# A scan and a mixture of adapters on one core: stores of two chunks in 4 KB rows, x stepped over the pair, fillers on TensorE, and new orders of all queues

## The chip, the cores and the metric

The kernel runs on one core of a Trainium2 chip. The metric is device time in microseconds (us) of one launch: the median of several runs. Five queues of instructions run beside each other and meet only through semaphores: PE (TensorE: matmuls, transposes), ACT (ScalarE), DVE (VectorE), POOL (GpSimd) and SP, which issues nearly all transfers. The transfers themselves run on 16 DMA engines.

## The reference

Two parts follow each other. The first is a linear recurrence along time, for 8 sequences of 6400 steps and 128 channels:

```python
for t in range(S):
    h = a[:, t] * h + b[:, t]
    out[:, t] = h
```

Its result, seen as 51200 tokens x of 128 numbers, goes through a mixture of 8 adapters of rank 16. A gate picks the two best adapters of each token, weighs them by a softmax over the two logits, and adds what they give:

```python
logits = x @ w_gate                          # 51200 x 8
topk = the two largest of each row; w = softmax of those two
delta[token] = sum over the two of w * ((x @ A[e]) @ B[e])
return x + delta
```

All inputs and the output are float32. a, b and the output have 26.2 MB each, so 78.6 MB have to pass between HBM and SBUF.

## The kernel before, in words

**Tiles.** The 51200 tokens are cut into 100 chunks of 512 tokens; a chunk has 4 blocks of 128 tokens. Loads fetch two chunks at a time (512 KB each for a and for b; the first four chunks come alone). A paired load gives each of the 128 partitions 8 tokens that follow each other in HBM, a row of 4 KB; a store of two chunks gives each partition 4 tokens of one chunk and 4 of the other, so it writes rows of 2 KB.

**One chunk's way.** Its steps carry short names in the planner, which also stand in this text:
- `la`, `lb`: loads of a and b (line 707), into rings of 6 pairs.
- `A`, `B`, `P` (line 728): PE transposes tokens into channels x time, in PSUM. `P` does b of one chunk and a of the next at once, with half of the rows of the array each.
- `ae` (line 746): ACT copies the transposed a to SBUF. `sc` (line 784): DVE runs the recurrence along the free axis and writes x, in half precision, to a ring of 24 chunks. These four are the front.
- `Z` (line 804): PE multiplies x with A and w_gate, in units of mostly 6 blocks. x is the weight operand: column 4p+j of a chunk belongs to partition p and block j, so the 128 weights of a block stand four halves apart. `ze` (line 810): ACT copies that to SBUF.
- Gating, in groups of mostly 4 units, on DVE, POOL and ACT (lines 841 to 880): the two largest logits, a sigmoid, the weights `g`.
- `mu` (line 913 on POOL, `md`, line 917, on DVE): z times the gate weights. `T` (line 926): PE transposes that. `te` (line 935 on DVE, 932 on ACT): a copy to SBUF. `D` (lines 940 and 941): PE adds x, again as weights with a step of four, and z B in PSUM. `oe` (line 955 on ACT, `od`, line 952, on DVE): a copy to the output ring of 18 chunks. `st` (line 986): SP stores a pair. These are the back.

**What sets the order.** Each engine works its own list from front to end and waits at an instruction until what that needs is done. The lists come from a planner in the kernel's file: each operation has an estimated duration and a wished-for time (the table `NUDGE`, one number for each operation), and the planner orders each engine's operations by that. Lists like `TE_ACT`, `MU_DVE` and `OE_DVE` say which of two engines does a step:

```python
rank[op.i] = op.base + TEMPLATE... + NUDGE.get(op.name, 0.0)
queue = {e: sorted((o for o in self.ops if o.eng == e), key=lambda o: (rank[o.i], o.i)) for e in self.ENGINES}
```

Fronts run ahead of backs, by some 16 to 20 chunks in the middle of the run. Loads stand ahead of stores on SP: the last load, `lb98`, is issued when stores up to `st62` have been issued, and the rest of the stores follow it. At the start PE transposes the identity 16 times (`wu`, line 611); the table `FILL`, for more such work before some fronts, is empty.

Of the kernel before, what the change touches and what calls it, by code (L numbers as in the profile page):

```python
# [10 lines left out]
PERIOD = 6  # L11
FREE = {"pe": 0.0, "act": 0.105, "dve": 0.082, "pool": 0.044, "sp": 0.0}
SEEN = {"pe": 0.06, "act": 0.04, "dve": 0.055, "pool": 0.08, "sp": 0.0}
SELF = {"pe": 0.0, "act": 0.035, "dve": 0.035, "pool": 0.078, "sp": 0.0}
PE_WAIT = 0.08
PE_FREE = 0.1
SP_MARGIN = 2.0
LAND_MARGIN = 1.0
Q_RATE = {3: 4.2e-3, 5: 2.1e-3, 7: 2.1e-3}
SCAN_SELF = 0.13  # L20
ISSUE = {"sp": 0.52, "act": 0.45}
LOAD_RATE = 387e3
STORE_RATE = 413e3
DMA_START = 0.3
DMA_SEEN = 1.15
DMA_DEPTH = 9
FIRST_ISSUE = 0.7
FIRST_WORK = 0.73
TABLES = 1.32
NUDGE = {  # L30
# [182 lines left out]
}  # L213
WINDOW = {'pe': 0.0, 'act': 0.0, 'dve': 0.0, 'pool': 0.0, 'sp': 0.0}
START = (-999, "", 0)
FIRST = -9999
EARLY = -400
LEAD = [1, 2]
# [4 lines left out]
FLAT = []  # L223
FILL = {}
# [70 lines left out]
class Program:  # L295
# [5 lines left out]
    def __init__(self):  # L301
        self.ops = []
# [802 lines left out]
```

## Time and profile before

| what | number |
|---|---|
| median of 3 runs | 202.84 us (202.61 to 203.44) |
| span of the profiled execution, first to last instruction | 200.9 us; the page gives no other time of that execution |
| busy: PE, DVE, ACT, POOL | 177.7, 176.2, 175.8, 136.9 us |
| moved between HBM and SBUF | 52.56 MB read, 26.21 MB written |
| packets on the main queue | 28456 |

The span lies 1.9 us under the median of the runs: it leaves out what is done around the program. Busy times of PE are modelled, and a busy PE is not PE at its peak. The DMA share can be over 1, as packets of one engine overlap.

### The profile page before, as it was taken

What the parts mean: (1) busy time and instruction counts of PE and PEld (TensorE: products, weight loads), DVE (VectorE), ACT (ScalarE), POOL (GpSimd) and SP (SyncE); (2) the same over time, 40 slices, a digit from 0 to 9 for tenths busy, and PEclk for the clock granted to TensorE, in tenths of its full rate; (3) what the DMA queues carried; (4) which work ended last, traced back from release to release, by engine and by line L of the source; (5) the groups of instructions that cost most, each with busy time, mean ns of one, the idle gap of its engine ahead of it and who ended that gap; (6) DMA issues with size and microseconds to landing.
All of it is one profiled execution on the core that took longest, in us unless ns stands there. A gap on an engine that the chain in (4) does not pass through costs nothing.

```text
span 200.9 us, 7611 instructions
## 1 busy us (share of the span) xinstructions
PE 177.7 (88%) x3192; PEld 155.9 (78%) x3192; DVE 176.2 (88%) x283; ACT 175.8 (88%) x327; POOL 136.9 (68%) x176
## 2 busy tenths in 40 slices
PE   6888978999899969999988999899999997898970
PEld 6766867888688858888878888787888886787860
DVE  1699999999999968999897999798899998999971
ACT  2589998999779969999997999899999998899970
POOL 1331559498989887797987797868876466767420
PEclk9999999999999999999999999999999999999998
DMA  6999999999999999999999999999999999999985
GB/s 216 378 412 408 411 405 401 411 406 404 414 409 400 412 416 409 401 417 407 409 413 409 410 409 412 413 410 411 417 408 410 414 410 409 406 381 387 357 338 215
DMA packets 29065, 79.26 MB, mean 395 GB/s; under 512 B 2664, under 2 KB 2920, under 8 KB 29032
## 3 DMA queue, kind: packets, MB, share of 16 engines
q1 hardware_dynamic: 28456, 78.39, 99.0%
q8 instruction: 25, 0.41, 0.8%
q10 hardware_dynamic: 576, 0.40, 0.7%
q14 instruction: 8, 0.07, 0.1%
HBM read 52.56 MB, written 26.21 MB: 392 GB/s over the span
## 4 chain that ended last, share of the span: by engine, by line
DMA 33%; PE 27%; DVE 16%; ACT 15%; SPq 5%; issue 2%; DVEq 0%; ACTq 0%
DMA a_tm<-in_a_dram 26%; DVE xT L784 9%; DMA out_dram<-outt 7%; ACT zl L810 5%; PE pZ L804 5%; SPq L707 5%; PE pB L728 5%; PE pA L728 5%; ACT outt L955 4%; PE pO L940 4%; PE pO L926 4%; ACT a_st L746 4%; PE pO L941 3%; DVE zwT L935 2%; ACT zwT L932 2%
## 5 line engine op out<-in xcount | busy, mean ns | idle before, releaser
L784 DVE TENSOR_TENSOR_SCAN xT<-a_st,xT,pB 128x512 f16<-128x512 f32 x96 | 120.4, 1254 | 7.1 <-PE pA L728 4.3
L913 POOL TENSOR_TENSOR zw<-zl,g 128x512 f16<-128x512 f32 x88 | 92.7, 1067 | 27.9 <-DVE g L880 19.6
L728 PE MATMUL pB<-ident_f,b_tm 64*128 64x64 f32 (+1 forms) x784 | 69.3, 229 | 6.8 <-DMA a_tm<-in_a_dram 6.7
L728 PE MATMUL pA<-ident_f,a_tm 64*128 64x64 f32 (+1 forms) x784 | 69.8, 230 | 0.5 <-DMA b_tm<-in_b_dram 0.3
L746 ACT COPY a_st<-pA 128x512 f32<-128x512 f32 x100 | 63.3, 638 | 4.1 <-PE pA L728 3.3
L728 PEld LDWEIGHTS pB<-ident_f,b_tm 64*128 64x128 f32 (+1 forms) x784 | 56.4, 139 | 11.8 <-DMA a_tm<-in_a_dram 8.3
L810 ACT COPY zl<-pZ 128x816 f32<-128x816 f32 (+1 forms) x69 | 59.7, 865 | 2.0 <-PE pZ L804 1.7
L728 PEld LDWEIGHTS pA<-ident_f,a_tm 64*128 64x128 f32 (+1 forms) x784 | 56.8, 139 | 5.6 <-issue 0.4
L955 ACT COPY outt<-pO 128x512 f32<-128x512 f32 x88 | 55.9, 640 | 3.9 <-PE pO L941 3.0
L940 PE MATMUL pO<-ident_h,xT 128*128 128x128 f16 x368 | 51.6, 222 | 1.3 <-ACT zwT L932 1.0
L941 PE MATMUL pO<-cst_h,zwT 128*128 128x128 f16 x368 | 50.5, 219 | 0.0
L940 PEld LDWEIGHTS pO<-ident_h,xT 128*128 128x128 f16 x368 | 40.2, 113 | 4.3 <-ACT zwT L932 1.4
L804 PE MATMUL pZ<-cst_h,xT 128*128 128x136 f16 x400 | 35.9, 225 | 4.9 <-DVE xT L784 2.0
L941 PEld LDWEIGHTS pO<-cst_h,zwT 128*128 128x128 f16 x368 | 36.8, 100 | 0.0
L926 PE MATMUL pO<-ident_h,zw 128*128 128x128 f16 x368 | 35.2, 220 | 1.4 <-ACT outt L955 1.1
L804 PEld LDWEIGHTS pZ<-cst_h,xT 128*128 128x128 f16 x400 | 26.3, 114 | 9.1 <-DVE xT L784 4.3
L926 PEld LDWEIGHTS pO<-ident_h,zw 128*128 128x128 f16 x368 | 22.9, 97 | 4.7 <-ACT outt L955 1.3
L935 DVE COPY zwT<-pO 128x512 f16<-128x512 f16 x57 | 22.9, 407 | 4.0 <-PE pO L926 3.7
L932 ACT COPY zwT<-pO 128x512 f16<-128x512 f16 x35 | 21.9, 630 | 4.7 <-PE pO L926 4.3
L850 POOL TENSOR_TENSOR L<-k,m 128x192 f32<-128x192 f32 (+2 forms) x16 | 8.4, 524 | 6.2 <-DVE m L848 6.1
L872 POOL TENSOR_TENSOR k<-k,L 128x192 f32<-128x192 f32 (+1 forms) x17 | 9.4, 556 | 4.3 <-DVE L L868 3.0
L846 POOL TENSOR_TENSOR L<-L,k 128x192 f32<-128x192 f32 (+1 forms) x15 | 8.6, 576 | 5.4 <-DVE L L843 4.7
(58 smaller groups left out, 112.2 us busy)
## 6 DMA issues: line engine op xcount, KB each, us to landing
a_tm<-in_a_dram SPq DMA_DIRECT2D x48, 512.0 KB, 13.3
b_tm<-in_b_dram SPq DMA_DIRECT2D x48, 512.0 KB, 13.5
out_dram<-outt SPq DMA_DIRECT2D x47, 512.0 KB, 13.4
a_tm<-in_a_dram SPq DMA_DIRECT2D x4, 256.0 KB, 4.3
out_dram<-outt SPq DMA_DIRECT2D x4, 256.0 KB, 3.6
b_tm<-in_b_dram SPq DMA_DIRECT2D x3, 256.0 KB, 5.1
out_dram<-outt SPq DMA_DIRECT2D x1, 496.0 KB
b_tm<-in_b_dram ACTq DMA_DIRECT2D x1, 256.0 KB, 3.4
```

Source lines behind the costliest of these rows:

```text
L728: last = eng["pe"].transpose(*args)
L746: lambda: eng["act"].copy(a_st[c % NA][:, :], pA[:, c % 2, :]), fr(c, "ae"))
L784: last = eng["dve"].tensor_tensor_scan(out=x[:, s0:s1], data0=a_st[c % NA][:, s0:s1], data1=pB[:, c % 2, s0:s1], initial=init, op0=ALU.mul ...
L804: last = eng["pe"].matmul(pZ[:, k // (n // 2), o : o + W], xblock(b0 + k), Awg_h)
L810: return eng["act"].copy(zl[:, zb : zb + n, :].rearrange("p (h k) w -> p h (k w)", h=2), pZ[:, :, 0 : n // 2 * W])
L913: lambda: eng["pool"].tensor_tensor(out=wv, in0=zv, in1=gv, op=ALU.mult), ba(gi, c, "mu"))
L926: last = eng["pe"].transpose(ptile[:, k * 128 : k * 128 + 128], zz[:, k, :], ident_h[:, :])
L932: lambda: eng["act"].copy(zt, ptile[:, 0 : n * 128]), ba(gi, c, "ta"))
L935: lambda: eng["dve"].tensor_copy(zt, ptile[:, 0 : n * 128]), ba(gi, c, "te"))
L940: eng["pe"].matmul(dst, xblock(b0 + k), ident_h[:, :], start=True, stop=False)
L941: last = eng["pe"].matmul(dst, zt[:, k * 128 : k * 128 + 128], B_h, start=False, stop=True)
L955: lambda: eng["act"].copy(ov, bv), ba(gi, c, "oe"))
```

## The change

The planner, its estimates, `NUDGE` and its switches go away. The order of each of the five lists is written out by name in a table `ORDER`, and the engine of a step is the one in whose list its name stands. Instructions, sizes of rings and units stay but for the points below; names of gate operations are `g` on every engine, and `mu`, `te`, `oe` on every engine.

```diff
-FILL = {}
+FILL = {k: 4 for k in range(7, 15)}
 ...
-            dst = out[r0 : r0 + m * C, :].rearrange("(h p j) d -> p h j d", p=128, j=J)
-            view = outt[:, q : q + m * J, :].rearrange("p (h j) d -> p h j d", j=J)
+            dst = out[c * C : (c + m) * C, :].rearrange("(p j) d -> p j d", p=128)
+            view = outt[:, q : q + m * J, :]
 ...
         def xblock(b):
-            return xcols(b // J).rearrange("d (p j) -> d j p", j=J)[:, b % J, :]
+            s0, n = tile_of[b // J]
+            o = s0 % NX * C
+            return xT[:, o : o + n * C].rearrange("d (p j) -> d j p", p=128)[:, b - s0 * J, :]
```

- **Stores.** A store of two chunks writes, from each partition, 8 tokens that follow each other: 128 rows of 4 KB instead of 256 of 2 KB. The last four chunks are still stored alone. Stores now use 16 semaphores in turn.
- **x over the pair.** For that, block j of a pair must hold the tokens 8p+j of its 1024. So the weights of `Z` and `D` are taken with a step of eight halves over the x of both chunks. `Z` therefore waits for the scan of the pair's second chunk, and the x of a pair is free again when `D` of both chunks has run.
- **Fillers.** Before the paired transposes that make a of chunks 7 to 14, PE transposes the identity four times into the place where that a goes:

```diff
+        def filler(c):
+            def f(e):
+                for _ in range(FILL[c]):
+                    last = e.transpose(pA[:, c % 2, 0:128], ident_f[:, :], ident_f[:, :])
+                return last
+            if c in FILL:
+                o_fi[c] = P.add("pe", f"fi{c}", FILL[c], get(o_ae, c - 2) + [o_id], f)
```

- **Orders.** All five lists are new. From SP's: near the start, and around the last load:

```diff
+    "sp": (
+        "la0 lb1 la1 la3 lb2 la2 lb3 la4 lb4 la6 lb6 ... la16 lb16 la18 lb20 lb18 la20 la24 la22 st0 lb22 ... "
+        "... st58 lb96 st60 la98 st62 st72 st64 lb98 st66 st68 st78 st76 st70 st74 st82 ... st94 st96 st97 st98 st99"
```

PE's end and those of ACT and DVE, from the last paired transpose `P98`, the last copy of a (`ae99`) and the last scan (`sc99`) on:

```diff
+    "pe":  "... T82 Z65 T83 D82 D83 T84 P98 T85 D84 Z66 D85 T86 B99 T87 Z67 T90 D86 ... D97 T99 D98 D99"
+    "act": "... te83 oe82 ze65 oe83 ae99 te85 oe84 ze66 oe85 w1_17 te86 te87 ... w1_21 te97 oe96 oe97 oe98 oe99"
+    "dve": "... mu88 sc98 g6_18 g7_17 mu90 g2_18 g8_17 sc99 mu94 te91 te88 gx_19 ... mu98 g8_21 mu99 te98 te99"
```

Before, the same places were: PE `P98 D83 D82 Z65 B99 T85 T84 Z66 ...`, ACT `oe83 oe82 ze65 ae99 ze66 oe85 ...`, DVE `sc98 te85 te84 g4_17 sc99 g1_18 g7_17 ...`.

By the two tables, DVE has 62 `te` (60 before), 5 `oe` (7), 10 `mu` (12) and ten gate operations more; ACT has 38 `te` (40) and 95 `oe` (93); POOL has 90 `mu` (88) and ten gate operations fewer.

More of the change, by code (lines that the diff above doesn't have):

```diff
@@ L302, in __init__, with add @@
         self.ops = []
-    def add(self, eng, name, dur, deps, emit, at, sem=None, locks=False, parts=1):
+        self.where = {name: e for e in ORDER for name in ORDER[e].split()}
+    def add(self, may, name, n, deps, emit, sem=None, parts=1):
         op = Op()
         op.i = len(self.ops)
-        op.eng, op.name, op.dur, op.emit = eng, name, dur, emit
-        op.base, op.kind, op.k = at
-        op.deps = [d for d in deps if d is not None]
-        op.sem, op.locks = sem, locks or eng == "pool"
-        op.cnt, op.clock, op.parts = 0, None, parts
+        op.may = may.split()
+        op.eng = self.where.get(name, op.may[0])
+        assert op.eng in op.may
+        op.name, op.n, op.emit = name, n, emit
+        op.deps = deps
+        op.sem, op.cnt, op.clock, op.parts = sem, 0, None, parts
@@ L393, in schedule @@
+    def schedule(self):
+        named = {op.name: op for op in self.ops}
+        assert len(named) == len(self.ops)
+        self.order = {e: [named[name] for name in ORDER[e].split()] for e in self.ENGINES}
+        assert sum(len(o) for o in self.order.values()) == len(self.ops)
         for e in self.ENGINES:
@@ L398, in schedule, with waits @@
                     op.cnt = n
-    def waits(self, sems, dma_sems):
+    def waits(self):
         dma_cnt = {}
@@ L411, in waits @@
                     op = self.order[e][at[e]]
-                    if any(d.clock is None for d, _ in op.deps):
+                    if any(d.clock is None for d in op.deps):
                         break
@@ L475, in bass_associative_scan_2x2__then__mixture_of_adapters_kernel @@
     NU = len(units)
-    GMAX = 4
-    stores = []
-    c0 = 0
-    for n in [2] * ((NCH - sum(STORE_TAIL)) // 2) + STORE_TAIL:
+    stores, tile_of, c0 = [], {}, 0
+    for n in STORES:
         stores.append((c0, n))
+        assert c0 % NX + n <= NX and c0 * J % NO + n * J <= NO
+        for c in range(c0, c0 + n):
+            tile_of[c] = (c0, n)
         c0 += n
     assert c0 == NCH
-    groups = []
-    u0 = 0
-    for n in LEAD + [GMAX] * ((NU - sum(LEAD) - sum(TAPER)) // GMAX) + TAPER:
+    groups, u0 = [], 0
+    for n in GROUPS:
         groups.append((u0, n))
@@ L490, in bass_associative_scan_2x2__then__mixture_of_adapters_kernel @@
     assert u0 == NU
-    bbase = []
-    for u0, n in groups:
-        e = (units[u0 + n - 1][0] + units[u0 + n - 1][1]) // J - PERIOD
-        bbase.append(max(e, bbase[-1] + PERIOD * last / GMAX) if bbase else e)
-        last = n
-    gfirst = [units[u0][0] // J for u0, n in groups]
     glast = [(units[u0 + n - 1][0] + units[u0 + n - 1][1]) // J - 1 for u0, n in groups]
@@ L552, in bass_associative_scan_2x2__then__mixture_of_adapters_kernel @@
         outt = sbuf("outt", [128, NO, 128], F32)
-        GB = GMAX * U
+        GB = max(sum(m for _, m in units[u0 : u0 + n]) for u0, n in groups)
         m1 = sbuf("m1_", [128, GB], F32, 2)
@@ L600, in bass_associative_scan_2x2__then__mixture_of_adapters_kernel @@
-        o_sg = P.add(
-            "act", "sg", TABLES + 0.2, [(o_id, True)],
-            lambda: eng["act"].activation(warm[:, :], ident_f[:, 0:E], ACTF.Sigmoid), START,
-        )
-        o_ih = P.add(
-            "dve", "ih", 0.25, [(o_id, True)],
-            lambda: eng["dve"].tensor_copy(ident_h[:, :], ident_f[:, :]), START,
-        )
-        o_wu = []
-        for k in range(WARM):
-            o_wu.append(P.add("pe", f"wu{k}", 0.218 if k < WARM0 else 0.109, [(o_id, True)],
-                  lambda: eng["pe"].transpose(pO[:, 0, 0:128], ident_f[:, :], ident_f[:, :]),
-                  START if k < WARM0 else (0, "wu", 0)))
@@ new lines, in bass_associative_scan_2x2__then__mixture_of_adapters_kernel @@
+        P.add("act", "sg", 0, [o_id], lambda e: e.activation(warm[:, :], ident_f[:, 0:E], ACTF.Sigmoid))
+        o_ih = P.add("dve", "ih", 0, [o_id], lambda e: e.tensor_copy(ident_h[:, :], ident_f[:, :]))
+        o_wu = [
+            P.add("pe", f"wu{k}", 0, [o_id],
+                  lambda e: e.transpose(pO[:, 0, 0:128], ident_f[:, :], ident_f[:, :]))
+            for k in range(WARM)
+        ]
+        o_ch = P.add("dve", "ch", 0, o_c[1:], lambda e: e.tensor_copy(cst_h[:, 128:], cst_f[:, 128:]))
@@ L727, in f @@
                     for args in group:
-                        last = eng["pe"].transpose(*args)
+                        last = e.transpose(*args)
                 return last
@@ L748, in front @@
-        def front(c):
-            r0 = rows[c]
-            o_fi = []
-            for k in range(FILL.get(c, 0)):
-                o_fi.append((P.add(
-                    "pe", f"fi{c}_{k}", 0.109, [(o_id, True)] + get(o_sc, c - 2),
-                    lambda: eng["pe"].transpose(pB[:, c % 2, 0:128], ident_f[:, :], ident_f[:, :]), fr(c, "fi")), True))
+            o_ae[c] = P.add("act", f"ae{c}", J, [o_A[c]] + get(o_sc, c - NA),
+                            lambda e: e.copy(a_st[c % NA][:, :], pA[:, c % 2, :]))
@@ new lines, in load_next, with f @@
+        def load_next(c):
+            if c < NCH and c not in o_la:
+                load(c, 1 if c < HEAD else HC)
+        o_fi = {}
+        def filler(c):
+            def f(e):
+                for _ in range(FILL[c]):
[3 more added lines that the diff above has]
+                o_fi[c] = P.add("pe", f"fi{c}", FILL[c], get(o_ae, c - 2) + [o_id], f)
+        def front(c):
+            load_next(c)
@@ L853, in maxes @@
-            def maxes():
-                for k in range(nb):
-                    last = eng["dve"].max(out=t8[:, k, :], in_=Lp[:, k, :])
-                return last
-            def first():
-                return eng["dve"].tensor_reduce(out=v1, in_=Lp, axis=X, op=ALU.max)
-            d1 = P.add("dve", f"g1_{gi}", 0.09 + 0.075 * nb if top else 0.142 + nb * E * 1.04e-3,
-                       [(o_ze[u], True) for u in range(u0, u0 + n)] + old, maxes if top else first, ga(gi, "g1"))
+                return P.add("dve" if kind == 8 else "pool dve", f"g{kind}_{gi}", nb, deps, f)
@@ L863, in gating @@
+            top = nb <= TOP8
+            ready = [o_ze[u] for u in range(u0, u0 + n)] + old
             if top:
+                t8 = v8[s][:, 0:nb, :]
                 b1, b2 = (t8[:, :, k : k + 1].to_broadcast([128, nb, E]) for k in (0, 1))
-                d2 = wide(2, [(d1, True)] + old,
-                          lambda e: e.tensor_tensor(out=kk, in0=Lp, in1=b1, op=ALU.subtract))
-                d5 = wide(6, [(d1, True)] + old,
-                          lambda e: e.tensor_tensor(out=ll, in0=Lp, in1=b2, op=ALU.subtract))
-            else:
-                d2, d5 = search()
@@ L871, in gating, with maxes @@
-            d6 = wide(7, [(d2, True), (d5, True)],
-                      lambda e: e.tensor_tensor(out=kk, in0=kk, in1=ll, op=ALU.add))
-            a1 = P.add("act", f"w1_{gi}", 0.19 + nb * E * 0.86e-3, [(d6, True)] + old,
-                       lambda: eng["act"].activation(sg, kk, ACTF.Sigmoid), ga(gi, "w1"))
+                def maxes(e):
+                    for k in range(nb):
+                        last = e.max(out=t8[:, k, :], in_=Lp[:, k, :])
+                    return last
+                d1 = P.add("dve", f"gx_{gi}", nb, ready, maxes)
@@ L875, in gating @@
+            d6 = wide(7, [d2, d5], lambda e: e.tensor_tensor(out=kk, in0=kk, in1=ll, op=ALU.add))
+            a1 = P.add("act", f"w1_{gi}", nb, [d6] + old, lambda e: e.activation(sg, kk, ACTF.Sigmoid))
             for u in range(u0, u0 + n):
@@ L899, in back_part @@
-        def back_part(gi, ch, c, b0, n):
             u0 = groups[gi][0]
+            b0 = c * J
             q0 = b0 - units[u0][0]
             w = c % NW
-            us = [u for u in range(u0, u0 + groups[gi][1]) if units[u][0] < b0 + n and units[u][0] + units[u][1] > b0]
-            gv = g[gi % NG][:, q0 : q0 + n, :].unsqueeze(3).broadcast_to([128, n, E, R])
+            us = [u for u in range(u0, u0 + groups[gi][1]) if units[u][0] < b0 + J and sum(units[u]) > b0]
+            gv = g[gi % NG][:, q0 : q0 + J, :].unsqueeze(3).broadcast_to([128, J, E, R])
@@ L918, in back_part @@
-            for k in range(n):
+            zv = zl[:, zp : zp + J, 0:128].rearrange("p q (e r) -> p q e r", e=E)
+            zz, zt = zw[w], zwT[w][:, :]
+            wv = zz[:, :, :].rearrange("p q (e r) -> p q e r", e=E)
+            o_mu[c] = P.add("pool dve", f"mu{c}", J, [o_ze[u] for u in us] + [o_g[gi]] + get(o_T, c - NW),
+                            lambda e: e.tensor_tensor(out=wv, in0=zv, in1=gv, op=ALU.mult))
+            for k in range(J):
                 zlast[zp + k] = o_mu[c]
@@ L922, in back_part @@
             ptile = bank.bitcast(F16)
-            def tr():
-                for k in range(n):
-                    last = eng["pe"].transpose(ptile[:, k * 128 : k * 128 + 128], zz[:, k, :], ident_h[:, :])
-                return last
-            o_T[c] = P.add("pe", f"T{c}", 0.1 + 0.056 * n, [(o_mu[c], True), (o_ih, True)] + free + [(o, True) for o in (o_wu if c < 2 else [])], tr, ba(gi, c, "T"))
-            if te_act(c):
-                o_te[c] = P.add("act", f"te{c}", 0.165 + 0.107 * n, [(o_T[c], True)] + get(o_D, c - NW),
-                                lambda: eng["act"].copy(zt, ptile[:, 0 : n * 128]), ba(gi, c, "ta"))
-            else:
-                o_te[c] = P.add("dve", f"te{c}", 0.14 + 0.0672 * n, [(o_T[c], True)] + get(o_D, c - NW),
-                                lambda: eng["dve"].tensor_copy(zt, ptile[:, 0 : n * 128]), ba(gi, c, "te"))
@@ L937, in delta, with tr @@
-            def delta():
-                for k in range(n):
+            def tr(e):
+                for k in range(J):
+                    last = e.transpose(ptile[:, k * 128 : k * 128 + 128], zz[:, k, :], ident_h[:, :])
+                return last
+            o_T[c] = P.add("pe", f"T{c}", J, [o_mu[c], o_ih] + free + (o_wu if c < 2 else []), tr)
+            o_te[c] = P.add("dve act", f"te{c}", J, [o_T[c]] + get(o_D, c - NW),
+                            lambda e: copy(e, zt, ptile[:, 0:C]))
@@ L939, in delta @@
+            def delta(e):
+                for k in range(J):
                     dst = bank[:, k * 128 : k * 128 + 128]
-                    eng["pe"].matmul(dst, xblock(b0 + k), ident_h[:, :], start=True, stop=False)
-                    last = eng["pe"].matmul(dst, zt[:, k * 128 : k * 128 + 128], B_h, start=False, stop=True)
-                return last
-            o_D[c] = P.add("pe", f"D{c}", 0.11 + 0.112 * n, [(o_te[c], True)], delta, ba(gi, c, "D"))
-            xlast[ch % NX] = o_D[c]
@@ L946, in back_part @@
-            o0 = b0 % NO
-            freed = {olast[o0 + k].i: olast[o0 + k] for k in range(n) if o0 + k in olast}
-            deps = [(o_D[c], True)] + [(x, True) for x in freed.values()]
-            ov, bv = outt[:, o0 : o0 + n, :].rearrange("p k w -> p (k w)"), bank[:, 0 : n * 128]
-            if c in OE_DVE:
-                o_oe[c] = P.add("dve", f"od{c}", 0.142 + 0.133 * n, deps,
-                                lambda: eng["dve"].tensor_copy(ov, bv), ba(gi, c, "oe"))
-            else:
-                o_oe[c] = P.add("act", f"oe{c}", 0.165 + 0.107 * n, deps,
-                                lambda: eng["act"].copy(ov, bv), ba(gi, c, "oe"))
@@ L956, in back_part @@
-            for k in range(n):
+                    e.matmul(dst, xblock(b0 + k), ident_h[:, :], start=True, stop=False)
+                    last = e.matmul(dst, zt[:, k * 128 : k * 128 + 128], B_h, start=False, stop=True)
+                return last
+            o_D[c] = P.add("pe", f"D{c}", J, [o_te[c]], delta)
+            s0, m = tile_of[c]
+            for k in range(s0, s0 + m):
+                if xlast.get(k % NX, (None, []))[0] != s0:
+                    xlast[k % NX] = (s0, [])
+                xlast[k % NX][1].append(o_D[c])
@@ L957, in back_part @@
+            o0 = b0 % NO
+            ov = outt[:, o0 : o0 + J, :].rearrange("p k w -> p (k w)")
+            o_oe[c] = P.add("act dve", f"oe{c}", J,
+                            [o_D[c]] + distinct(olast[o0 + k] for k in range(J) if o0 + k in olast),
+                            lambda e: copy(e, ov, bank[:, :]))
+            for k in range(J):
                 olast[o0 + k] = o_oe[c]
@@ L995, in store @@
+            op.deps += [o_st[-NS]] if len(o_st) >= NS else []
+            o_st.append(op)
             for k in range(m * J):
                 olast[q + k] = op
-        def store_half(ch, c, j):
-            q = (ch * J + j) % NO
-            n = J // 2
-            r0 = rows[ch]
-            dst = out[r0 : r0 + C, :].rearrange("(p j) d -> p j d", j=J)[:, j : j + n, :]
-            op = P.add(
-                "sp", f"st{c}", n * 128 * D * 4 / LOAD_RATE, [(o_oe[c], True)],
-                lambda: eng["sp"].dma_start(dst, outt[:, q : q + n, :]), (PERIOD * (ch // PERIOD), "st", ch % PERIOD // 2),
-                sem=dma_sem(f"stx{c % 4}"),
-            )
-            o_st[c] = op
-            for k in range(n):
-                olast[q + k] = op
@@ L1012, in load_next, with fronts @@
-        def load_next(c):
-            if c not in o_la:
-                load(c, 1 if c < HEAD else HC)
-        nf, nb = 0, 0
+        def fronts(c):
+            s0, n = tile_of[c]
+            return s0 + n
+        nf, nb, ns = 0, 0, 0
         for gi, (u0, n) in enumerate(groups):
@@ L1019, in bass_associative_scan_2x2__then__mixture_of_adapters_kernel @@
                 b0, m = units[u]
-                while nf * J < b0 + m:
-                    load_next(nf)
+                while nf < fronts((b0 + m - 1) // J):
                     front(nf)
@@ L1032, in bass_associative_scan_2x2__then__mixture_of_adapters_kernel @@
                 nb += 1
+                if sum(stores[ns]) == nb:
+                    store(*stores[ns])
+                    ns += 1
         P.schedule()
-        waits = P.waits(s_eng, s_dma)
+        waits = P.waits()
         def run(name, handle):
@@ L1045, in run @@
                 else:
-                    for part in inst if op.parts > 1 else [inst]:
+                    for part in inst if isinstance(inst, list) else [inst]:
                         part.then_inc(s_dma[op.sem], 16)
@@ L1053, in _ @@
             run("sp", sp)
-            final = {}
+            final = {op.sem: op.cnt for op in P.order["sp"] if op in o_st}
             for op in P.order["sp"]:
-                if op.sem.startswith("st"):
-                    final.pop(op.sem, None)
-                    final[op.sem] = op
-            for key in final:
-                sp.wait_ge(s_dma[key], 16 * sum(o.parts for o in o_st.values() if o.sem == key))
+                if op in o_st and op.cnt == final[op.sem]:
+                    sp.wait_ge(s_dma[op.sem], op.cnt)
         @block.gpsimd
```

443 lines of the change are left out of this document (109 added, 334 removed), and 244 rows, old and new, of tables (NUDGE, ORDER).

## The prediction

> **What bounds the kernel now.** I read the page first: engines, the slices of the span, the queues.
>
> ```profile
> span 200.9 us, 7611 instructions
> PE 177.7 (88%) x3192; PEld 155.9 (78%) x3192; DVE 176.2 (88%) x283; ACT 175.8 (88%) x327; POOL 136.9 (68%) x176
> DMA  6999999999999999999999999999999999999985
> q1 hardware_dynamic: 28456, 78.39, 99.0%
> HBM read 52.56 MB, written 26.21 MB: 392 GB/s over the span
> a_tm<-in_a_dram SPq DMA_DIRECT2D x48, 512.0 KB, 13.3
> b_tm<-in_b_dram SPq DMA_DIRECT2D x48, 512.0 KB, 13.5
> out_dram<-outt SPq DMA_DIRECT2D x47, 512.0 KB, 13.4
> ```
>
> PE, DVE and ACT each show 88%, so none of them stands out; the DMA slices are at nine and above from 5 to 195 us, and a transfer lands some 13 us after its issue. Then I asked for the stages.
>
> ```profile
> core 0: us, PE busy (x) PEld busy (x) DVE busy (x) ACT busy (x) POOL busy (x), PEclk, DMA share, GB/s
> 10.00:24.00 14.00, 11.96 (x223) 9.99 (x221) 13.63 (x20) 12.46 (x24) 4.83 (x8) 1.00 1.03 410
> 44.00:104.00 60.00, 56.14 (x1052) 49.36 (x1051) 55.38 (x78) 55.43 (x104) 51.32 (x63) 1.00 1.03 409
> 104.00:164.00 60.00, 56.21 (x1062) 49.61 (x1064) 55.09 (x80) 57.20 (x107) 44.84 (x54) 1.00 1.03 411
> 180.00:185.00 5.00, 4.36 (x65) 3.68 (x64) 5.00 (x21) 4.92 (x12) 3.89 (x5) 1.00 1.04 396
> 185.00:190.00 5.00, 4.90 (x80) 4.29 (x79) 4.13 (x19) 4.45 (x10) 2.53 (x8) 1.00 0.92 355
> 190.00:195.00 5.00, 3.69 (x60) 3.18 (x58) 4.41 (x11) 3.91 (x9) 1.36 (x3) 1.00 0.91 340
> 195.00:201.00 6.00, 0.87 (x16) 0.69 (x13) 1.02 (x2) 0.74 (x2) 0.00 (x0) 0.88 0.60 230
> ```
>
> Up to 164 us the DMA share is 1.03 whatever else runs (over 1, since packets of one DMA engine overlap): transfers are the bound there, while ACT and DVE keep 5 to 8% idle. After 185 us the share is 0.92, then 0.60, and the rate falls: there the stores wait for the arithmetic. So there are two places to price: bytes per us in the long stretch, and the tail from the last load to the last copy. The clock is granted in full throughout, so it is no term.
>
> **The change part by part.**
>
> *Stores of 4 KB rows.* A pair of chunks was 256 rows of 2 KB; it becomes 128 rows of 4 KB, the form that the paired loads have. 48 of the 52 stores change, 25.2 of the 26.2 MB.
>
> ```profile
> 24.97 0.40 SPq L986 DMA_DIRECT2D out_dram<-outt  x1
> ```
>
> No row shows a 4 KB store. The near rows are these: 10 to 24 us holds loads of 4 KB alone at 410 GB/s, since the first store is issued at 25 us; 104 to 164 us mixes them with 2 KB stores at 411. By that the short rows cost nothing: bound 0. The other bound is 180 to 185 us, which moves stores alone: 396 GB/s at share 1.04, so 381 per unit of busy time, against 410/1.03 = 398 for 4 KB loads. 25.2 MB at 381 are 66.1 us, at 398 63.3: a gain of 2.8 us. Below nothing I go by 0.3 us only, since the same engines carry 4 KB rows at 410 in the same trace. The stretch with stores alone is the only one in which their price stands by itself, but it is short; I take the middle, **-1.4 us**.
>
> [...]
>
> *x stepped over the pair.* Column 8p+j instead of 4p+j feeds Z (line 804) and D (line 940) as weights; the count of instructions stays.
>
> ```profile
> L804 PEld LDWEIGHTS pZ<-cst_h,xT x400: 110/113/134, 8.3 to 183.7; 128*128 128x128 f16 x134
> L940 PEld LDWEIGHTS pO<-ident_h,xT x368: 111/113/116, 15.3 to 191.0; 128*128 128x128 f16 x184
> L926 PEld LDWEIGHTS pO<-ident_h,zw x368: 95/98/99, 12.6 to 188.9; 128*128 128x128 f16 x184
> ```
>
> Weights in a row take 98 ns, at a step of four halves 113: +15 for two doublings. One more doubling costs +7 if each costs the same, +20 if the price follows the step (15 ns for 6 bytes, 8 more bytes). At 800 such loads that is 6 to 16 us of PEld, but beside matmuls: PEld is busy 82% in 44 to 164 us. I take 0 on the path; cover gone, it is a rival. Z also has to await the scan of the pair's second chunk, up to one scan of 1.28 us later for every other chunk. The x ring of 24 chunks stands against a D some 16 to 20 chunks behind its front in both orders; nothing waits: 0.
>
> *Fillers.* Eight groups of four 128x128 f32 transposes ahead of fronts 7 to 14. Such a group starts 0.44 us after the one before it:
>
> ```profile
> 5.46 0.60 PE L728 MATMUL pB<-ident_f,b_tm 128*128 128x128 f32 x4
> 5.90 0.60 PE L728 MATMUL pA<-ident_f,a_tm 128*128 128x128 f32 x4
> ```
>
> 8 x 0.44 = 3.5 us, where PE has 2.0 us idle in 14 and DVE is busy 13.63 of 14. Up to 1.5 us would push fronts back, and the transposes, ACT copies and scans behind them. DVE orders that stretch, and ten transfers stand in the queues (13.3 us at 410 GB/s), so DMA does not run dry: 0, with +1.5 as the far end. The clock is granted in full already: nothing to win.
>
> *Orders: SP.* Its waits run in line, so a load placed early (lb20 ahead of lb18) holds all behind it, but only a hold of more than the 13 us in flight would empty the queues: 0 in the stretch. What counts is what stands before the last load.
>
> ```profile
> 162.58 1.77 SPq L707 DMA_DIRECT2D b_tm<-in_b_dram  x1
> 164.39 33.59 SPq L986 DMA_DIRECT2D out_dram<-outt  x21
> ```
>
> Behind lb98 now stand 21 of 53 store issues (one pair is split in two), 32 pairs before it. The new order has 34 before it (st64 and st72 were added): 1.05 MB at 410 = +2.6 us, less 34/48 of 1.4 = 1.0 for cheaper stores: lb98 lands about 1.6 us later. It landed near 162.58 + 13.5 = 176.1.
>
> *Orders: who does what.* By the two orders POOL has 90 multiplies for 88 and 70 small gate operations for 80, DVE 10 multiplies for 12, 5 outt copies for 7, 62 zwT copies for 60 and the ten gate operations; ACT gives up two zwT copies and takes two outt copies.
>
> ```profile
> L913 POOL TENSOR_TENSOR zw<-zl,g 128x512 f16<-128x512 f32 x88 | 92.7, 1067 | 27.9 <-DVE g L880 19.6
> L850 POOL TENSOR_TENSOR L<-k,m 128x192 f32<-128x192 f32 (+2 forms) x16 | 8.4, 524 | 6.2 <-DVE m L848 6.1
> ```
>
> POOL: 2 x 1.07 - 10 x 0.52 = -3.1 us on an engine at 68%; DVE: with the durations that stand below for its tail, 4 x 0.68 - 2 x 0.42 = 1.9 us less for copies and multiplies, and ten gates more, mostly the small ones of the last groups, that take it back. In sum 0; what counts is when.
>
> *Orders: the tail.* Three rows of the chain of waits and two of the timeline:
>
> ```profile
> 176.62 0.20 PE pB L728
> 181.63 1.19 DVE xT L784
> 195.91 0.69 DVE outt L952
> ```
> ```profile
> 177.19 0.62 PE L926 MATMUL pO<-ident_h,zw 128*128 128x128 f16 x8
> 180.53 0.65 ACT L746 COPY a_st<-pA 128x512 f32<-128x512 f32 x1
> ```
>
> The last paired transpose P98 follows two transposes of older chunks (T83, T82) at 177.8, its copy ae99 goes at 180.53, two us after P98's end, behind older copies; the last scan ends at 182.8, and the last copy 13.8 us after that. What DVE and ACT have behind these points:
>
> ```profile
> L917 DVE TENSOR_TENSOR zw<-zl,g 128x512 f16<-128x512 f32 x7 | 4.7, 683 | 0.0
> L935 DVE COPY zwT<-pO 128x512 f16<-128x512 f16 x4 | 1.7, 420 | 0.9 <-PE pO L926 0.9
> L952 DVE COPY outt<-pB 128x512 f32<-128x512 f32 x1 | 0.7, 683 | 0.0
> L855 DVE MAX8 v<-zl 128x8 f32<-128x8 f32 x15 | 1.3, 151 | 0.0
> ```
> ```profile
> L955 ACT COPY outt<-pO 128x512 f32<-128x512 f32 x8 | 4.6, 589 | 0.6 <-PE pO L941 0.6
> L932 ACT COPY zwT<-pA 128x512 f16<-128x512 f16 x3 | 1.8, 594 | 0.0
> ```
>
> Counted in the two orders after sc99, DVE has 5 multiplies instead of 7, no outt copy instead of 3, 9 zwT copies instead of 7, 4 MAX8 fewer and one small gate operation more: -2 x 0.68 - 3 x 0.68 + 2 x 0.42 - 4 x 0.15 + 0.2 = -3.0 us. ACT after ae99 has 3 outt copies more and one zwT copy less: 3 x 0.59 - 0.6 = +1.2 us. Both are as good as full in that stretch, so the end moves by something between +1.2 (ACT sets it) and -3.0 (DVE does); the mean of both, -0.9, is what an even split gives, and I take it. The late landing counts against this: of 1.6 us I take half, +0.8, since ae99 now stands two us behind its transposes and the new order has less old work before it. The tail: **-0.1 us**, ends +2.8 and -3.0. The last store itself is the same.
>
> *The sum.* 200.9 - 1.4 - 0.1 = 199.4 us of span. Runs of this kernel have a median 1.9 us above the profiled span (202.84 against 200.9), so 201.3. The engines have to follow a pace 0.7% quicker; ACT, the fullest, is idle for 2.8 of 60 us in 104 to 164 us, so they can.
>
> **The rivals.**
>
> *Faster still: stores at 398, DVE's tail.* -2.8 for the stores; lb98 then lands only 2.6 - 34/48 x 2.8 = 0.6 us later, half of it counts, and half of DVE's 3.0 comes off: -1.2. 198.8 us. For it: the stores-alone row; against it: 411 in the mix. Chance 0.22.
>
> *No gain from rows.* The mixed row holds, 0 for the stores; then lb98 lands 2.6 us later, half of that against -0.9 in the tail: +0.4, 203.2. Chance 0.18.
>
> *Slower: the last load and ACT.* lb98 behind two more stores, its whole 1.6 us passed on to ae99, and 1.2 us more for ACT behind it: +2.8, 205.6 (the cheaper stores are in the 1.6 already). It decides as soon as ae99 starts later than about 181.5 us. For it: ACT 4.92 of 5 us in 180 to 185; against it: DVE holds most of the chain of waits there. Chance 0.14.
>
> *Slower: weights of x on PE's path.* 800 loads x 20 ns = 16 us, less the idle of PE (120 - 112.4 = 7.6 us in 44 to 164, some 10 in all): +6, 208.8 without, 207.4 with the stores' gain. It decides from 15 ns of each load unhidden (7.6 us over 8 loads for each of 65 chunks). Against it: a load is hidden by the matmul before it. [...] Chance 0.08.
>
> *The forecast* keeps 0.38, its own range 200.3 to 202.3.
>
> **How the numbers follow.** 0.5% is 1.0 us, so faster is below 201.8, slower above 203.9; that is about what a measurement of this kernel can tell. Faster: 0.22 and three quarters of 0.38, with a little of the third case: 0.53. Slower: 0.14 + 0.08, and a fifth of the case without a gain: 0.26. Same: 0.21. The range must leave out no more than 2 in 10: from 198.8, the quick rival, to 204.3, which leaves out the dear end of the ACT rival and the weights.
>
> **What will show it.** Right: some 6,100 packets fewer in q1 (48 x 128) with the same MB; the DMA share still 1.03 in the middle but the rate at 413 or more; stores alone above 400 GB/s; the weights of x at lines that answer to 804 and 940 near 120 to 133 ns with PE no busier than 94%; the last scan near 182 and the last copy 12 to 13 us after it, with ACT full. Wrong: a rate of 411 with the long rows; stretches with a share below 0.95 before 175 us (SP held, or the arithmetic behind); weights of x far over 133 ns with PE without idle; the last a/b transposes after 179.5 us.

## The result, and the profile after

| | before | after |
|---|---|---|
| median of the runs | 202.73 us (4 runs) | 201.22 us (4 runs, 201.01 to 201.50) |
| span of the profiled execution | 200.9 us | 199.2 us |

The ratio is 0.9921, with a 95% interval from 0.9897 to 0.9945. The prediction was 201.3 us. In one of the runs below, the one with half stores and a step of four, two of four executions were slow, more than 1.5% above the fastest, and only the other two are compared.

The page of the changed kernel, the lines that answer to those of before:

```profile
span 199.2 us, 7709 instructions
PE 185.2 (93%) x3224; PEld 165.5 (83%) x3224; DVE 175.0 (88%) x291; ACT 176.9 (89%) x327; POOL 136.0 (68%) x168
q1 hardware_dynamic: 22312, 78.39, 98.1%
PE 80%; ACT 5%; DMA 4%; issue 3%; SPq 2%; POOL 2%; DVE 1%; DVEq 0%
out_dram<-outt SPq DMA_DIRECT2D x47, 512.0 KB, 11.9
```

The main queue has 28456 - 22312 = 6144 packets fewer for the same MB, exactly 48 x 128. DVE and ACT are as busy as before, PE by 7.5 us more. The fourth line, the shares in the chain of work that ended last, is new: 80% of it is PE's. Of before, DMA had 33% of that chain and PE 27%. The share of q1, the main queue, is worth a sum: 99.0% of 200.9 us are 198.9 us, 98.1% of 199.2 are 195.4. The packets took 3.5 us less of a DMA engine's time, in the mean of the 16; the kernel's time fell by 1.5.

The stages of the changed kernel; the columns are those of the table of before:

```profile
10.00:24.00 14.00, 13.59 (x212) 11.29 (x211) 13.48 (x25) 10.23 (x20) 0.84 (x4) 1.00 1.03 411
44.00:104.00 60.00, 56.98 (x1074) 51.74 (x1076) 55.14 (x78) 56.20 (x104) 47.47 (x58) 1.00 1.03 412
104.00:164.00 60.00, 58.56 (x1096) 53.13 (x1094) 57.15 (x84) 58.04 (x107) 50.32 (x61) 1.00 1.03 412
180.00:185.00 5.00, 4.97 (x76) 4.59 (x76) 5.00 (x12) 5.00 (x11) 2.53 (x4) 1.00 0.94 380
185.00:190.00 5.00, 4.90 (x80) 4.55 (x78) 4.82 (x25) 5.00 (x13) 3.07 (x5) 1.00 0.78 311
190.00:195.00 5.00, 4.00 (x60) 3.24 (x57) 3.28 (x14) 4.14 (x10) 0.47 (x1) 1.00 1.02 404
```

In the long stretch the same DMA share of 1.03 now moves 412 GB/s, not 409 and 411. The change is half a percent in a column that is easily passed over. The stretch with loads alone, 10 to 24 us, stays where it was (411, before 410). From 190 to 195 us stores run alone with full queues: 404 at 1.02, or 396 per unit of busy time, where 2 KB rows gave 396 at 1.04, or 381. Between 185 and 190 us the share falls to 0.78, where it was 0.92 before: a hole in the transfers.

### The profile page after: what moved, and what is told of

The parts are those of the page before. It is cut to its first block, busy times and chain, and to the rows that moved or that the text cites. A ratio compares the mean times of both kernels' runs of the same rounds, so it can differ in the third digit from the quotient of the medians.

```text
span 199.2 us, 7709 instructions
## 1 busy us (share of the span) xinstructions
PE 185.2 (93%) x3224; PEld 165.5 (83%) x3224; DVE 175.0 (88%) x291; ACT 176.9 (89%) x327; POOL 136.0 (68%) x168
## 3 DMA queue, kind: packets, MB, share of 16 engines
q1 hardware_dynamic: 22312, 78.39, 98.1%
## 4 chain that ended last, share of the span: by engine, by line
PE 80%; ACT 5%; DMA 4%; issue 3%; SPq 2%; POOL 2%; DVE 1%; DVEq 0%
PE pB L417 23%; PE pO L588 13%; PE pZ L500 13%; PE pO L578 12%; PE pO L589 10%; PE pA L417 5%; DMA a_tm<-in_a_dram 4%; ACT outt L300 3%; PE pA L446 2%; SPq L396 2%; POOL zw L569 2%; ACT zwT L300 1%; ACT a_st L435 1%; ACT zl L506 1%; DVE xT L482 1%
## 5 line engine op out<-in xcount | busy, mean ns | idle before, releaser
L417 PE MATMUL pA<-ident_f,a_tm 64*128 64x64 f32 (+1 forms) x784 | 67.8, 229 | 0.6 <-issue 0.4
L435 ACT COPY a_st<-pA 128x512 f32<-128x512 f32 x100 | 59.0, 613 | 7.9 <-PE pA L417 7.2
L588 PE MATMUL pO<-ident_h,xT 128*128 128x128 f16 x368 | 55.2, 233 | 2.0 <-issue 1.8
L300 ACT COPY outt<-pO 128x512 f32<-128x512 f32 x87 | 52.2, 609 | 4.6 <-PE pO L589 4.1
L589 PE MATMUL pO<-cst_h,zwT 128*128 128x128 f16 x368 | 53.0, 219 | 1.7 <-issue 1.7
L588 PEld LDWEIGHTS pO<-ident_h,xT 128*128 128x128 f16 x368 | 46.3, 144 | 4.9 <-issue 2.1
L589 PEld LDWEIGHTS pO<-cst_h,zwT 128*128 128x128 f16 x368 | 39.6, 108 | 1.8 <-issue 1.8
L500 PEld LDWEIGHTS pZ<-cst_h,xT 128*128 128x128 f16 x400 | 30.6, 145 | 1.5 <-DVE cst_h L324 0.2
L545 POOL TENSOR_TENSOR L<-L,k 128x192 f32<-128x192 f32 x14 | 8.8, 631 | 4.6 <-DVE L L543 4.0
L482 DVE TENSOR_TENSOR_SCAN xT<-a_st,pB 128x512 f16<-128x512 f32 (+1 forms) x8 | 7.5, 938 | 4.5 <-PE pB L417 4.4
## 6 DMA issues: line engine op xcount, KB each, us to landing
a_tm<-in_a_dram SPq DMA_DIRECT2D x48, 512.0 KB, 13.3
```

The lines of the kernel that those rows point to most:

```text
L300: return e.copy(dst, src) if e is eng["act"] else e.tensor_copy(dst, src)
L417: last = e.transpose(*args)
L435: lambda e: e.copy(a_st[c % NA][:, :], pA[:, c % 2, :]))
L482: last = e.tensor_tensor_scan(out=x[:, s0:s1], data0=a_st[c % NA][:, s0:s1], data1=pB[:, c % 2, s0:s1], initial=init, op0=ALU.mult, op1=AL ...
L500: last = e.matmul(pZ[:, k // (n // 2), o : o + W], xblock(b0 + k), Awg_h)
L545: d3 = wide(5, [d3], lambda e: e.tensor_tensor(out=ll, in0=ll, in1=kk, op=ALU.add))
```

## The experiments

**Which part brings the gain?** Four kernels take the parts asunder. In three of them x and the store rows are set one by one; fillers and orders stay as in the changed kernel. The fourth leaves the fillers out.

Both undone:

```diff
-            return xT[:, o : o + n * C].rearrange("d (p j) -> d j p", p=128)[:, b - s0 * J, :]
+            return xcols(b // J).rearrange("d (p j) -> d j p", j=J)[:, b % J, :]
...
-            dst = out[c * C : (c + m) * C, :].rearrange("(p j) d -> p j d", p=128)
-            view = outt[:, q : q + m * J, :]
+            dst = out[c * C : (c + m) * C, :].rearrange("(h p j) d -> p h j d", p=128, j=J)
+            view = outt[:, q : q + m * J, :].rearrange("p (h j) d -> p h j d", j=J)
```

> The changed kernel with its orders, fillers and waits, but x taken with a step of four over one chunk and stores in 2 KB rows, as before the change. Theory A (the prediction: the rows are worth 1.4 us, the step of the weights is hidden): 202.6 us. Theory B (the rows are worth more, and the slower weights of x take part of it back, some 1 us): 201.6 to 202.6. Theory C (rows and step do nothing, the orders alone bring the gain): 201.2. In all of them the weights of x go back to 113 ns.

Measured: 202.41 us beside 202.71 of the kernel before; ratio 0.9989, interval 0.9972 to 1.0005. Theory C falls; A and B both allow this time.

The first of these two edits alone (step of four, rows of 4 KB):

> The changed kernel with 4 KB store rows, but x taken with a step of four over one chunk. Left out: the order of tokens in the output (within a pair they land at wrong rows), so the time is that of the same work. Theory A: 201.2, as the changed kernel, with weights of x at 113 ns and PE busy 1.5 to 2 us of 60 less in the middle. Theory B: 200.2 or lower, since PE, busy 58.56 of 60 us at 104 to 164, gets free. Theory C: 201.2.

Measured: 201.09 us, ratio 0.9923 (0.9901 to 0.9946). Theory B, which needed 200.2 or lower, falls.

The second alone (step of eight, rows of 2 KB):

> The changed kernel with x stepped over the pair, but stores in 2 KB rows. Left out: the order of tokens in the output (within a pair they land at wrong rows). Theory A: 202.6, the rows alone being worth 1.4 us; the rate at 104 to 164 us falls from 412 to about 410 GB/s. Theory B: 202.6 or more. Theory C: 201.2, the same rate.

Measured: 202.36 us, ratio 0.9990 (0.9965 to 1.0015).

| us | rows of 2 KB | rows of 4 KB |
|---|---|---|
| step of four | 202.41 | 201.09 |
| step of eight | 202.36 | 201.22 (the changed kernel) |

Down a column nothing happens; across a row 1.1 to 1.3 us go. The 201.22 was measured in another round than the other three; as ratios to the kernel before of the same round the two gains are 0.66 and 0.69%, or 1.3 and 1.4 us. The rows are the gain, as theory A had it, and the step costs nothing that a time shows. What is left for orders and fillers is the ratio 0.9989, whose interval holds 1. The chain of work that ended last does not follow the time here: PE has 51% of it with a step of four and rows of 4 KB (201.09 us) and 80% with a step of eight (201.22). The stages at 104 to 164 us, first with step of eight and 2 KB rows, then with step of four and 4 KB rows, each from its own kernel:

```profile
104.00:164.00 60.00, 57.98 (x1080) 52.47 (x1078) 56.40 (x84) 57.67 (x106) 49.59 (x60) 1.00 1.03 410
```
```profile
104.00:164.00 60.00, 57.23 (x1087) 50.75 (x1084) 56.34 (x85) 57.64 (x107) 49.93 (x60) 1.00 1.03 413
```

The last column follows the rows (410, 413), the first the step (57.98, 57.23).

**The fillers.** `FILL = {}`, and the eight names out of PE's list:

> The changed kernel without the eight groups of fillers. Prediction: 201.2, no difference, since DVE orders that stretch and DMA does not run dry. Rival (fillers push the fronts back, far end 1.5 us): 199.7 to 201.2. Other rival (they hold PE's clock through late landings): slower, over 201.7, with a granted clock or spacing of transposes that is worse at 10 to 30 us.

Measured: 201.48 us, ratio 0.9947 (0.9927 to 0.9968). That interval overlaps the changed kernel's, so no difference is shown, as predicted. At 10 to 24 us, where the fillers stand, PE's busy time is what moved:

```profile
10.00:24.00 14.00, 11.55 (x190) 9.46 (x191) 13.41 (x25) 10.44 (x20) 0.81 (x3) 1.00 1.03 411
```

It is 11.55 instead of 13.59; the clock is granted in full with and without them (1.00 in both rows).

**The rows under the old orders.** In the kernel before:

```diff
-            dst = out[r0 : r0 + m * C, :].rearrange("(h p j) d -> p h j d", p=128, j=J)
-            view = outt[:, q : q + m * J, :].rearrange("p (h j) d -> p h j d", j=J)
+            dst = out[r0 : r0 + m * C, :].rearrange("(p j) d -> p j d", p=128)
+            view = outt[:, q : q + m * J, :]
```

> The kernel before, its orders and its step of four, with stores in 4 KB rows. Left out: the order of tokens in the output (within a pair they land at wrong rows). If the rows are worth the same under these orders: 201.3 to 201.5. If they help only where the order of the queues can use it: 202 to 202.7.

Measured: 201.45 us beside 202.78; ratio 0.9930 (0.9906 to 0.9955). The rows are worth 1.3 us under the old lists too.

**Is the last load what the end waits for?** The sum of the prediction charged the two stores ahead of `lb98`. Put behind it:

```diff
-... la98 st62 st72 st64 lb98 st66 st68 st78 st76 st70 ...
+... la98 st62 lb98 st72 st64 st66 st68 st78 st76 st70 ...
```

> The changed kernel with lb98, the last load, put ahead of st72 and st64 on SP; the rest of the order as it is. Theory A (the last load sets the last scan, and the tail behind it is a fixed stretch of work, so the 2.6 us of the sum were right): the last paired transpose and the last scan go 1.5 to 2.5 us earlier, the time falls to 199.2 to 200.2. Theory D (transfers as a whole set the end, the same bytes being moved): the scan goes earlier, the time stays at 201.2.

Measured: 201.39 us, ratio 0.9947 (0.9923 to 0.9970): no gain. The timelines, first SP's in the changed kernel and then in this one, show that the edit did move the load:

```profile
158.68 6.11 SPq L631 DMA_DIRECT2D out_dram<-outt  x3
164.83 0.45 SPq L396 DMA_DIRECT2D b_tm<-in_b_dram  x1
```
```profile
159.96 1.06 SPq L396 DMA_DIRECT2D b_tm<-in_b_dram  x1
163.48 4.12 SPq L631 DMA_DIRECT2D out_dram<-outt  x5
```

It goes out 4.9 us earlier. In the changed kernel it lands at 178.2 us, 13.3 us after its issue; in this one no load took more than 17.2 us from issue to landing, so it has landed by 177.2 us. PE, in the changed kernel and then in this one:

```profile
178.92 0.40 PE L578 MATMUL pO<-ident_h,zw 128*128 128x128 f16 x4
179.25 0.28 PE L417 MATMUL pB<-ident_f,b_tm 64*128 64x64 f32 x1
```
```profile
179.15 0.40 PE L578 MATMUL pO<-ident_h,zw 128*128 128x128 f16 x4 [0.71 <-ACT outt L300]
179.47 0.27 PE L417 MATMUL pB<-ident_f,b_tm 64*128 64x64 f32 x1
```

The last paired transpose P98 stays at 179.3 to 179.5, more than 1 us after the load has landed in either kernel. Both times it follows directly on T84, the transpose that stands before it in PE's list, and in the second kernel the bracket says whom T84 waited for: a copy on ACT. The load is there; the list is late. Theory A's mechanism falls. Theory D's expectation that the scan would go earlier falls too.

**SP's holds.** The 6.11 us row above is three stores: SP stood 4.2 us at `st72`, whose second chunk was copied to the output ring only by 163.9 us. `st64` stood behind it, with both of its chunks copied by 150.2 us. SP stands in the same way at `st78` (6.1 us), `st82` (2.3) and `st86` (3.4). In the order in which they are ready, first with two stores ahead of `lb98`, then with none:

```diff
-... la98 st62 st72 st64 lb98 st66 st68 st78 st76 st70 st74 st82 st80 st86 st84 st90 st88 st92 ...
+... la98 st62 st64 st66 lb98 st68 st70 st72 st74 st76 st78 st80 st82 st84 st86 st88 st90 st92 ...
```

> The changed kernel with the stores from st62 on in the order in which their chunks are ready (st64, st66, then lb98, then st68, st70 and so on), so that SP is no longer held for st72, st78, st82 and st86 while older pairs lie ready; two stores stand ahead of lb98 as before. Theory D (the hole at 185 to 190 us, DMA share 0.78, and the 0.94 before it are SP's holds, and transfers set the end): shares of about 1.03 until 190 us, and 1.2 to 1.7 us less: 199.5 to 200. Theory A (the arithmetic behind the last load sets the end): holes gone, the time 200.9 to 201.2.

Measured: 201.60 us, ratio 0.9942 (0.9922 to 0.9962).

> Both: lb98 directly behind st62, and the stores behind it in the order in which they are ready. Theory A: as the early load alone, 199.2 to 200.2. Theory D: as the ready order alone, 199.5 to 200. If both the arithmetic and the transfers have to be early: less than either, 198.8 to 199.5.

Measured: 201.84 us, ratio 0.9951 (0.9933 to 0.9969). Neither is better than the changed kernel, and no theory had this: D's times are missed in both, A expected the holes gone in the first and 199.2 to 200.2 us in the second, and the third case (198.8 to 199.5) is missed too. The hole is still there, in the first and in the second:

```profile
164.00:176.00 12.00, 11.26 (x190) 9.92 (x192) 10.74 (x18) 11.42 (x22) 9.98 (x11) 1.00 1.03 415
185.00:190.00 5.00, 4.90 (x81) 4.60 (x79) 4.82 (x26) 5.00 (x13) 3.08 (x5) 1.00 0.78 311
```
```profile
185.00:190.00 5.00, 4.93 (x82) 4.63 (x80) 4.82 (x24) 5.00 (x13) 2.82 (x5) 1.00 0.74 298
```

The earlier stores did go earlier (415 GB/s at 164 to 176 us, 405 in the changed kernel), and then none was left for 185 to 190 us, where PE, DVE and ACT are all full (4.8 to 5.0 of 5 us). In the changed kernel, whose share there is 0.78 too, SP waited 3.4 us, until 185.25, for ACT's copy to the output ring. So SP's order does not make the hole; the arithmetic has no finished chunk to hand over. Nor does a fuller stretch alone buy time. With a step of four and rows of 4 KB, under SP's order of the changed kernel, it reads:

```profile
185.00:190.00 5.00, 4.88 (x86) 4.62 (x84) 4.88 (x29) 4.73 (x13) 2.88 (x5) 1.00 0.95 380
```

That kernel took 201.09 us against 201.22. Each of these rows is one execution.

**How far behind is the arithmetic?** Each store cut to its first 64 partitions takes 13.1 MB off the transfers. In the changed kernel, and likewise in the one before:

```diff
-                return [e.dma_start(dst[p : p + n], view[p : p + n]) for p, n in zip(lows, cuts)]
+                return [e.dma_start(dst[0:64], view[0:64])]
```

> The changed kernel with each store cut to its first 64 partitions (and st68 no longer split). Left out: half of the output, 13.1 MB of the 78.6 that the transfers move, some 32 us of their time; the arithmetic is whole. Theory F (transfers bind until 175 us, the arithmetic has 3 to 6% to spare, as the prediction took it): 193 to 197 us. Theory G (the arithmetic binds as well since the rows are cheaper, as the last paired transpose did not move with an earlier last load): 199.5 to 201.

Measured: 197.79 us, ratio 0.9729 (0.9690 to 0.9767).

> The same half stores, and x taken with a step of four over one chunk. Left out: half of the output, and the order of tokens in the rest. With the transfers out of the way the weights of x (143 against 113 ns, 800 loads) show what they cost on PE: if they stay hidden by matmuls, the same as with a step of eight within 0.5 us; if PE is what the arithmetic waits for, up to 800 x 30 ns = 24 us less, by PE's busy times 3 to 4 us less.

Measured: 196.52 and 198.63 us, ratio 0.9739 (0.9661 to 0.9817). The question that this run was for, what the step costs when transfers are out of the way, stays open: the intervals cover each other, and the profiled spans (197.2 with eight, 196.0 with four) are single executions.

> The kernel before with each store cut to its first 64 partitions (st68 not split). Left out: half of the output. The arithmetic's own time under the old orders and a step of four: Theory F: 193 to 197, as with the new orders; theory G: 199.5 to 201. Under the new orders with a step of four it should be the same if the orders are worth nothing beside the stores, shorter if they are better where arithmetic binds.

Measured: 196.44 us, ratio 0.9690 (0.9639 to 0.9740). The old orders come down into theory F's range; with the new ones neither F nor G has its number.

How much do half stores take off the transfers? Three lines of the changed kernel with half stores, one of its page and two stages:

```profile
q1 hardware_dynamic: 18992, 65.28, 89.7%
104.00:164.00 60.00, 59.40 (x1110) 54.01 (x1109) 57.45 (x87) 58.73 (x109) 50.99 (x61) 1.00 0.92 363
190.00:196.00 6.00, 3.04 (x43) 2.29 (x40) 2.31 (x6) 3.42 (x8) 0.00 (x0) 1.00 0.94 198
```

89.7% of a span of 197.2 us are 176.9 us of packets, against 195.4 with whole stores: 18.5 us less, not the 32 us expected. Stores of 64 partitions alone moved 198 GB/s at a share of 0.94, or 211 per unit of busy time, where whole ones moved 396. With the old orders the long stretch even stays full:

```profile
104.00:164.00 60.00, 58.46 (x1108) 51.62 (x1105) 57.47 (x84) 59.13 (x110) 46.82 (x57) 1.00 1.00 380
```

So these runs do not show the arithmetic by itself. They show that it can end at least 3.4 us sooner with the new orders (201.22 to 197.79) and 6.4 us sooner with the old ones (202.87 to 196.44). With the new orders the share at 104 to 164 us is down to 0.92 and PE is busy 59.40 of 60 us, so more than the transfers holds that stretch; that it is PE is not shown.

## Why the prediction was right, point by point

**Rows of 4 KB: right in mechanism and in size.** Predicted 1.4 us, measured 1.1 to 1.3 (202.41 to 201.09 is 1.3, 202.36 to 201.22 is 1.1, 202.78 to 201.45 is 1.3). That the middle of two bounds came so near is in part luck, as nothing in the rows before said where between them the gain would lie. Of the two bounds, 0 from the mixed row and 2.8 from the stretch of stores alone, neither was right by itself. The mixed row hid the price: 411 and 410 GB/s agree to a quarter of a percent, but stores are a third of the bytes, and 1.2 us in 200 are 0.6% of the rate. The stretch of stores alone showed what a store takes of the engines (381 before, 396 after the change), and q1's packets did take 3.5 us less in all; but the time got only a part of that. Where the rest went is open. The rate in the middle was said to reach 413 or more; it reached 412. Why rows of 2 KB take more of the engines' time for the same bytes is not shown; what the page shows is 6144 packets fewer and 3.5 us less of the packets' time.

**The step of x: right that it is hidden, wrong in the size of a load.** The weight loads of the changed kernel:

```profile
L500 PEld LDWEIGHTS pZ<-cst_h,xT x400: 111/144/172, 11.7 to 184.7; 128*128 128x128 f16 x134
L588 PEld LDWEIGHTS pO<-ident_h,xT x368: 141/143/148, 20.4 to 190.6; 128*128 128x128 f16 x184
```

The term took +7 to +20 ns by drawing on from 98 and 113; it is +30: 98, 113, 143 for steps of one, four and eight halves. A step of eight is not one more doubling of the same price. Why it takes 30 ns more is not shown. The prediction set 15 ns unhidden for each load as the point where PE decides. 30 ns came, and the two kernels with the two steps are 201.09 and 201.22 us. So with whole stores the loads are as good as hidden. The prediction's sign of being wrong, weights far over 133 ns with PE without idle, came near (58.56 of 60 us, where it had named 94% as the limit). That reading was wrong: a busy PE was not yet a slower kernel.

**Fillers, and who does what.** The prediction put both at 0, and no run shows a difference: 201.48 us without the fillers beside 201.22, and orders and fillers together a ratio of 0.9989 whose interval holds 1.

**The last load: the step that failed.** "lb98 lands about 1.6 us later", of which half was to reach the last scan. It landed 1.3 us later (162.58 + 14.3 = 176.9 before, 164.83 + 13.3 = 178.2). The last scan did come later, and by the whole 1.6 us. The last two scans on DVE, in the timeline of the changed kernel:

```profile
180.78 1.27 DVE L482 TENSOR_TENSOR_SCAN xT<-a_st,xT,pB 128x512 f16<-128x512 f32 x1
183.10 1.28 DVE L482 TENSOR_TENSOR_SCAN xT<-a_st,xT,pB 128x512 f16<-128x512 f32 x1
```

The last one ends at 184.38, against 182.82 before (181.63 + 1.19). But the run with an early `lb98` has its last scan at 183.34, no sooner, with the load out 4.9 us sooner: PE's and ACT's lists hold the scan, not the transfer. So the landing was sized about right, but the path from it to the end, which the sum charged with 0.8 us, is not there, and a remedy built on it bought nothing.

**The tail: mis-sized, and less tied to the time than the sum took it.** From the last scan's end to the last copy's end it was 13.8 us; the mean of -3.0 (DVE sets it) and +1.2 (ACT sets it) gave -0.9. The last copies of the changed kernel:

```profile
193.67 1.17 ACT L300 COPY outt<-pB 128x512 f32<-128x512 f32 x2 [0.23 <-PE pB L589]
```

They end at 194.84, 10.5 us after the scan's end at 184.38: -3.3 us, DVE's end of the bounds. Scan and tail together bring the last copy 1.8 us forward (196.60 to 194.84), where the sum had 0.1. Yet the kernel with rows of 2 KB and the rest of the change, whose last copy ends before 195 us as well (ACT and DVE are busy 0.00 us at 195 to 199 us), gains next to nothing (202.36 us, ratio 0.9990). So a copy that ends earlier is not a store that ends earlier. After the hole at 185 to 190 us the transfers run with full queues again (1.02 at 190 to 195 us). The net of 0.1 for the tail was right for the time by luck: the late scan and the short tail were both mis-sized, and what they left over did not reach the time.

**The pace: "they can".** They could. How much was to spare is open: with half stores the changed kernel came down to 197.8 us, with the DMA engines still busy for 176.9 us of it, so the arithmetic's own time is at most that.

**The rivals.** Faster still: its price for stores came (396 per unit of busy time), its time of 198.8 us did not. No gain from rows: shown wrong by the table of four. Weights on PE's path: not so with whole stores, open without. The last load and ACT: it was to decide from an `ae99` later than about 181.5 us, and `ae99` began at 180.0.

## What to carry to other kernels

When transfers are saturated over the whole run, half a percent in the GB/s column can be the whole gain of a change: here 409 and 411 became 412, and the time fell by 1.5 us. Price a row length from a stretch in which that kind of transfer runs alone, but take that as an upper bound: here it gave 2.8 us, and the time fell by 1.1 to 1.3. Before charging a late load, look which instruction stands in front of the waiting one in its engine's list: two timelines with the load at two times decide it. When bytes are left out to see the arithmetic, look first what the DMA engines' time became: here a sixth of the bytes was a tenth of it. And in this kernel, with the transfers full and three engines busy 88 to 93% of the span, new orders moved waits about and not the end.

## What had not been expected

A f16 weight load of 128 columns took 98, 113 and 143 ns at steps of one, four and eight halves (medians of L926 and L940 of the kernel before and of L588 of the changed one), and 800 loads of 30 ns more left the time as it was. Half stores of 64 partitions took a sixth of the bytes away and only 18.5 of 195.4 us of the packets' time. The kernels with half stores take 196.4 us under the old orders and 197.8 under the new ones: the new lists are not shown to be the shorter ones there (the intervals, 0.9639 to 0.9740 and 0.9690 to 0.9767, overlap, and the two kernels also differ in step and row length).
